# Linear attention feeding a GELU feed-forward layer: rests of two batches by head, w_out in long runs, v's cast ahead of q's last copies

## The chip, the cores and the metric

The kernel runs on one core of a Trainium2 chip. The metric is device microseconds of one execution. The kernel before took 294.98 us (median of five runs, 293.32 to 297.63). The profiled execution took 293.32 us, of which 291.54 us are the span that the trace covers.

## The reference

There are 8 batches with 8 heads, 576 tokens and a head size of 64, all in float32. Per batch and head:

```python
phi(x) = where(x > 0, x, exp(x) - 1) + 1          # = min(max(x + 1, 1), exp(x)) here
kv  = phi(k).T @ v                                  # 64 x 64
z   = sum over tokens of phi(k)                     # 64
att = (phi(q) @ kv) / (phi(q) @ z + 1e-6)
x   = att of all heads side by side                 # 4608 x 512
h   = x @ w_in                                      # w_in 512 x 2048
out = gelu_tanh(h) @ w_out                          # w_out 2048 x 512
```

The kernel leaves out the 1e-6 and computes in bfloat16 with float32 sums.

## The kernel before

**Tokens.** The 576 tokens of a batch are cut into 512 main tokens, four per partition (`C = 4`), and a rest of 64 (`REST`). Two batches share one 128-partition tile for their rests: the even batch has partitions 0 to 63, the odd one 64 to 127 (`load_rest_half`, L77). A rest is loaded with the token on the partition and the heads side by side, which in memory are runs of 64 floats, 256 bytes. Main tokens come in runs of four tokens, 1 KB (`load_main`, L65).

**kv.** Per pair of heads `kv_mm` (L222) adds five products into PSUM: four of the main chunks and one of the rest, whose v tile `vrs` is zero outside its batch's half. v carries a column of ones (`E = D + 1 = 65`), so z comes along. `kv_evac` (L243) copies the two diagonal blocks of each pair into a block-diagonal tile `kvbd`. `nab_mm` and `nab_evac` multiply q with it and divide; `t_x` transposes the result into `xt`, features on the partitions.

**Feed-forward.** The main tokens of one batch make one feed-forward pass `j` (L784), and the rests of all batches together a ninth. `first_half(j)` computes 16 feature tiles of h (`first_mm`, L307), each followed by a gelu on ScalarE into `g`; `second_half(j)` computes out from `g` and `w_out_sb` in 16 steps of four matmuls. The feature on partition p of tile m is column 128 m + p of w_in, and row 128 m + p of w_out. Both weights are loaded in float32, in 1-MB chunks of 512 features, and cast to bfloat16 mostly by POOL in halves (`cast_w_in_halves` L148, `cast_w_out_halves` L155); each w_out chunk arrives as four 2-KB runs per partition.

**Order.** The schedule is written by hand: the order in the program is the order on each engine. Work of the next batches is put into slots of `first_half` and `second_half` by `at(phase, j, slot, fn)`; a function runs behind the slot's matmuls (`fill`, L697 and L756). All plain loads ahead of the steady state go out on SP's queue, into six buffers of the pool `pld`, so a load waits until the earlier user of its buffer is done. PSUM tiles of one bank come from `ps_ho` (four), those of two banks from `ps_a` (two, taken in turn).

**The head.** Batch 0 has code of its own, L324 to L420. ScalarE computes the exponentials in halves of four heads, DVE the phi (`phi_line`, `phi_min`), TensorE the transposes of q in four pairs (`transpose_q`), with matmuls on a zero tile between (`keep_warm`). The v casts follow the last q copies, half on DVE and half on ScalarE; then kv, the products, and the first h tiles in quarters of 128 tokens.

**Batch 1** is prepared inside pass 0 by `plan_second` (L537): exponentials on ScalarE after feature tile 11, phi and v's cast on DVE at the start of the second half, q's transposes in slot 8 (first copy on ScalarE, second on DVE), kv in slot 10, the products from slot 11. The last four gelus of pass 0 stand behind these exponentials on ScalarE.

Of the kernel before, what the change touches and what calls it, by code (L numbers as in the profile page):

```python
# [15 lines left out]
def kernel(  # L16
# [40 lines left out]
    w_in_r = moe_w_in.rearrange("(c p) f -> p c f", p=P)  # L57
    w_out_r = moe_w_out.rearrange("(m p) f -> p m f", p=P)

# [37 lines left out]
    def load_w_out(i):  # L97
        t = pld.tile([P, 4, 512], FP32, name="w_st", tag="ld")
        nc.sync.dma_start(out=t, in_=w_out_r[:, 4 * i : 4 * i + 4, :])
        return t  # L100
# [14 lines left out]
    nc.scalar.preload_act_table_set("exp_and_others")  # L115
    for n, src in (("k", k), ("q", q)):
        ld[n, 0] = load_main(src, 0, n + "_x", nc.sync, parts=2)
    for n in ("kr", "vr", "qr"):
        ld[n, 0] = prest.tile([P, H, D], FP32, name=n[0] + "_r")
    load_rest_half(k, ld["kr", 0], 0, 0, nc.sync)  # L120
    load_rest_half(v, ld["vr", 0], 0, 0, nc.sync)
    ld["v", 0] = load_main(v, 0, "v_x", nc.sync, parts=2)
# [11 lines left out]
    ]  # L134
    kvbds = [const.tile([P, NP, 2 * E], BF16, name=f"kvbd{i}") for i in range(4)]
    for i in range(2):
        nc.gpsimd.memset(vps[i][:, :, :, D:E], 1.0)
        for s in range(2):
            nc.gpsimd.memset(vrs[i][s], 0.0)
            nc.gpsimd.memset(vrs[i][s][REST * s : REST * (s + 1), :, D:E], 1.0)  # L140
        nc.gpsimd.memset(kvbds[i], 0.0)
# [6 lines left out]
    def cast_w_in_halves(i):  # L148
        for u in range(2):
            nc.gpsimd.tensor_copy(  # L150
                out=w_in_sb[:, :, 512 * i + 256 * u : 512 * i + 256 * (u + 1)],
                in_=w_st[i][:, :, 256 * u : 256 * (u + 1)],
            )
# [47 lines left out]

    def exp_rest_half(name, e, s):
        r = slice(REST * s, REST * (s + 1))
        exp_into(e[r], ld[name, 0][r])

    def phi_rest_half(name, e, s):
        r = slice(REST * s, REST * (s + 1))
        phi_line(phi[name, 0][r], ld[name, 0][r])
        phi_min(phi[name, 0][r], e[r])

    def cast_v(b, fn, s=slice(0, H)):
# [5 lines left out]
    def cast_vr(m, halves=(0, 1)):  # L217
        for s in halves:
            r = slice(REST * s, REST * (s + 1))
            nc.vector.tensor_copy(out=vrs[m % 2][s][r, :, 0:D], in_=ld["vr", m][r])  # L220

    def kv_mm(b, i, kv_ps, at_i=None):  # L222
        i_ps = i if at_i is None else at_i
        kp = phi["k", b].rearrange("p c h d -> p c (h d)")
        kr = phi["kr", b // 2].rearrange("p c h d -> p c (h d)")
        dst = kv_ps[:, i_ps // 2, 2 * E * (i_ps % 2) : 2 * E * (i_ps % 2) + 2 * E]
        for c in range(C):
            nc.tensor.matmul(  # L228
                dst,
                lhsT=kp[:, c, P * i : P * (i + 1)],  # L230
                rhs=vps[b % 2][:, 2 * i : 2 * i + 2, c, :],
                start=(c == 0),
                stop=False,
            )
        nc.tensor.matmul(  # L235
            dst,
            lhsT=kr[:, 0, P * i : P * (i + 1)],
            rhs=vrs[(b // 2) % 2][b % 2][:, 2 * i : 2 * i + 2, :],
            start=False,
            stop=True,  # L240
        )

    def kv_evac(b, kv_ps, bank=None, second=None):  # L243
# [4 lines left out]
        for hf in range(2):  # L248
            r, u = slice(64 * hf, 64 * hf + 64), slice(E * hf, E * hf + E)
            fn = second if hf and second else nc.vector.tensor_copy  # L250
            fn(out=dst[r, :, :, u], in_=src[r, :, :, u])  # L251
# [73 lines left out]
    qe = pe.tile([P, C, H, D], BF16, name="q_e")  # L325
    kre = pe.tile([P, 1, H, D], BF16, name="kr_e")
    kp = pphi.tile([P, C, H, D], BF16, name="k_p")
    qp = pphi.tile([P, C, H, D], BF16, name="q_p")
    phi["k", 0], phi["q", 0] = kp, qp
    phi["kr", 0] = pphi.tile([P, 1, H, D], BF16, name="kr_p")  # L330
    nc.gpsimd.memset(phi["kr", 0][REST:P], 0.0)
    qt = pt.tile([P, C, NP, P], BF16, name="qt")
# [7 lines left out]

    def transpose_q(i, copy):
        src = q_src(0)
        t_ps = ps_ho.tile([P, C, 2, P], BF16, name="t_ps", tag="ho")
        for c in range(C):
            nc.tensor.transpose(t_ps[:, c, 0, :], src(c, i), ident)
        copy(out=qt[:, :, i, :], in_=t_ps[:, :, 0, :])

    for n, e in (("k", ke), ("q", qe)):
        for s in halves:
            exp_into(e, ld[n, 0], s)  # L350
    exp_rest_half("kr", kre, 0)
    keep_warm(36)
    for n, xp, e in (("k", kp, ke), ("q", qp, qe)):
        for s in halves:
            phi_line(xp, ld[n, 0], s)
            phi_min(xp, e, s)
    for i in range(2):
        transpose_q(i, nc.scalar.copy)
    keep_warm(5)
    phi_rest_half("kr", kre, 0)  # L360
    cast_vr(0, (0,))
    for i in range(2, NP):
        transpose_q(i, nc.scalar.copy if i == 2 else nc.vector.tensor_copy)
    keep_warm(2)
    for h in range(2):
        cast_v(0, nc.vector.tensor_copy, slice(4 * h, 4 * h + 2))
        cast_v(0, nc.scalar.copy, slice(4 * h + 2, 4 * h + 4))
    for h in range(2):
        kv_ps = ps_a.tile([P, 2, 512], FP32, name="kv_ps", tag="a")
        for i in range(2):  # L370
            kv_mm(0, 2 * h + i, kv_ps, i)
        kv_evac(0, kv_ps[:, 0:1], h, nc.scalar.copy)
    keep_warm(1)
# [54 lines left out]
    ld["k", 1] = load_main(k, 1, "k_x", nc.sync)  # L428
    load_rest_half(k, ld["kr", 0], 0, 1, nc.sync)
    wo_st.append(load_w_out(2))  # L430
    load_rest_half(v, ld["vr", 0], 0, 1, nc.sync)
    ld["v", 1] = load_main(v, 1, "v_x", nc.sync)
# [104 lines left out]
    def plan_second():  # L537
# [4 lines left out]
        def exps():  # L542
            box["q"] = pe.tile([P, C, H, D], BF16, name="q_e")
            for s in halves:
                exp_into(box["q"], ld["q", b], s)
            box["k"] = exp_main("k", b)
            box["kr"] = pe.tile([P, 1, H, D], BF16, name="kr_e")
            exp_rest_half("kr", box["kr"], 1)
            gelu_table()

        def phis():
# [4 lines left out]
            phi["k", b] = phi_of(ld["k", b], box["k"], "k_p")  # L556
            phi_rest_half("kr", box["kr"], 1)

        def cast_vs():
            cast_vr(0, (1,))  # L560
            cast_v(b, nc.vector.tensor_copy)
# [8 lines left out]
        def kv():  # L570
            kv_ps = ps_a.tile([P, 2, 512], FP32, name="kv_ps", tag="a")
            for i in range(NP):
                kv_mm(b, i, kv_ps)
            kv_evac(b, kv_ps)

        def tq(h):
# [3 lines left out]
            t_q(q_src(b), None, 2 * h, 2, t_ps)  # L580
            copy = nc.vector.tensor_copy if h else nc.scalar.copy
            copy(out=box["qt"][:, 2 * h : 2 * h + 2], in_=t_ps[:, 0:2])

# [15 lines left out]
        for fn, c, slot in (  # L599
            (tq, 0, 8), (tq, 1, 8), (lambda c: kv(), 0, 10), (lambda c: last_w_out(), 0, 10),  # L600
            (nab, 0, 11), (nab, 1, 12), (nab, 2, 13), (tx, 0, 13), (nab, 3, 14),
# [213 lines left out]
```

## Time and profile before

| what | value |
|---|---|
| median of five runs | 294.98 us |
| profiled execution | 293.32 us |
| its span | 291.54 us |
| TensorE matmuls busy | 283.5 us (97%) |
| ScalarE busy | 157.9 us (54%) |
| DVE busy | 115.1 us (39%) |
| POOL busy | 36.2 us (12%) |
| granted TensorE clock | full in all 40 slices |
| moved by DMA | 53.75 MB, mean 184 GB/s |

Times in views are microseconds from the start of the span. PE is TensorE's matmuls, PEld its weight loads, ACT ScalarE, POOL GpSimd, SP the queue that issues most loads. A timeline line gives start, length, engine, line of the code, operation, tiles and count, and in brackets how long the engine had been idle before and what released it. A matmul's recorded length is a latency: 512-column matmuls follow each other in about 0.216 us, though each is recorded with some 0.38. A busy TensorE is therefore read from its waits.

### The profile page before, as it was taken

The page shows a single profiled execution, that of the slowest core. Times are in us where ns is not written, and L with a number is a line of the kernel's source. Part 1 is how long each engine was busy: PE and PEld are TensorE (multiplying, and loading weights), DVE is VectorE, ACT ScalarE, POOL GpSimd, SP SyncE. Part 2 cuts the span into 40 slices and gives each one's busy share as a digit, 9 for nine tenths or more (in the row PEclk, how much of TensorE's full clock was granted, in tenths as well). Part 3 has the DMA queues.
Part 4 walks back from the last instruction along what each step waited for, and adds up shares of the span by engine and source line. Part 5 has one row for each costly group of instructions (what it writes and reads, how often), then busy time and mean ns, then how long its engine had stood idle before and what let it go on. Part 6 is the DMA issues. An engine that isn't in the chain of part 4 may idle for free.

```text
span 291.5 us, 4277 instructions
## 1 busy us (share of the span) xinstructions
PE 283.5 (97%) x1693; PEld 149.4 (51%) x1722; DVE 115.1 (39%) x187; ACT 157.9 (54%) x219; POOL 36.2 (12%) x56
## 2 busy tenths in 40 slices
PE   8999999999999999999999999999999999999994
PEld 6885446645565545544454445444544444444443
DVE  3760586146683792447035642462240000000012
ACT  4647684589855753566356925672551076026400
POOL 8057338400007000000000000000000000000000
PEclk9999999999999999999999999999999999999999
DMA  6999999995389995998923894305150110020032
GB/s 238 355 406 397 367 365 382 342 366 159 68 262 215 323 196 150 290 255 291 329 56 70 296 266 112 72 3 160 53 74 18 72 74 0 31 94 21 0 72 72
DMA packets 65907, 53.75 MB, mean 184 GB/s; under 512 B 33888, under 2 KB 58720, under 8 KB 65888
## 3 DMA queue, kind: packets, MB, share of 16 engines
q1 hardware_dynamic: 62464, 42.35, 52.2%
q10 hardware_dynamic: 2464, 8.52, 7.5%
q0 software_dynamic: 960, 2.62, 3.0%
q8 instruction: 13, 0.21, 0.3%
q14 instruction: 6, 0.05, 0.0%
HBM read 36.70 MB, written 9.44 MB: 158 GB/s over the span
## 4 chain that ended last, share of the span: by engine, by line
PE 84%; DMA 7%; SPq 5%; POOL 1%; issue 1%; DVE 1%; DVEq 0%
PE o_ps L738 39%; PE h_ps L310 38%; DMA w_st<-in_moe_w_in_dram 4%; DMA w_st<-in_moe_w_out_dram 3%; PE n_ps L262 3%; PE kv_ps L228 2%; SPq L78 2%; SPq L69 2%; PE o_ps L707 1%; SPq L92 1%; POOL w_in_sb L150 1%; PE kv_ps L235 1%; POOL w_out_sb L157 0%; PE t_ps L285 0%; PE t_ps L256 0%
## 5 line engine op out<-in xcount | busy, mean ns | idle before, releaser
L738 PE MATMUL o_ps<-w_out_sb,g 128*128 128x512 bf16 x547 | 123.3, 379 | 1.0 <-POOL w_out_sb L157 0.3
L310 PE MATMUL h_ps<-xt,w_in_sb 128*128 128x512 bf16 (+2 forms) x574 | 118.5, 351 | 0.8
L695 ACT ACTIVATE g<-h_ps 128x512 bf16<-128x512 f32 x144 | 84.1, 598 | 49.4 <-PE h_ps L310 48.0
L738 PEld LDWEIGHTS <-g 128*128 128x128 bf16 x560 | 54.2, 98 | 63.6 <-issue 0.5
L310 PEld LDWEIGHTS <-w_in_sb 128*128 128x128 bf16 x652 | 59.1, 98 | 53.6 <-issue 0.3
L753 ACT COPY o_sb<-o_ps 128x512 f32<-128x512 f32 x18 | 10.5, 586 | 58.4 <-PE o_ps L738 58.4
L751 DVE COPY o_sb<-o_ps 128x512 f32<-128x512 f32 x17 | 11.7, 689 | 66.3 <-PE o_ps L738 59.0
L274 DVE TENSOR_TENSOR x<-n_ps,r 128x512 bf16<-128x512 f32 x36 | 24.9, 692 | 1.2
L251 DVE CAST kvbd<-kv_ps 64x260 bf16<-64x260 f32 (+1 forms) x16 | 6.6, 410 | 36.7 <-PE kv_ps L235 36.6
L169 ACT ACTIVATE k_e<-k_x 128x2048 bf16<-128x2048 f32 (+1 forms) x9 | 15.5, 1719 | 4.7 <-DMA k_x<-in_k_dram 4.7
L272 DVE RECIPROCAL r<-n_ps 128x8 f32<-128x8 f32 x36 | 7.4, 206 | 24.9 <-PE n_ps L262 24.9
L169 ACT ACTIVATE q_e<-q_x 128x2048 bf16<-128x2048 f32 (+1 forms) x10 | 15.5, 1559 | 2.5 <-DMA q_x<-in_q_dram 2.5
L186 DVE TENSOR_TENSOR k_p<-k_p,k_e 128x2048 bf16<-128x2048 bf16 (+1 forms) x9 | 10.0, 1106 | 12.3 <-ACT k_e L169 12.0
L180 DVE TENSOR_SCALAR q_p<-q_x 128x2048 bf16<-128x2048 f32 (+1 forms) x10 | 11.6, 1156 | 8.0 <-DMA q_x<-in_q_dram 7.9
L337 PE MATMUL w_ps<-warm 128*128 128x252 bf16 x94 | 13.4, 306 | 1.1 <-DVE warm L128 1.1
L310 PE MATMUL h_ps<-xt_rest,w_in_sb 128*128 128x512 bf16 x62 | 13.9, 379 | 0.1
L262 PEld LDWEIGHTS <-qt 128*128 128x128 bf16 x128 | 9.8, 98 | 7.5 <-DVE kvbd L251 0.6
L262 PE MATMUL n_ps<-kvbd,qt 128*128 128x130 bf16 x128 | 12.7, 221 | 0.4 <-ACT kvbd L251 0.2
L186 DVE TENSOR_TENSOR q_p<-q_p,q_e 128x2048 bf16<-128x2048 bf16 (+1 forms) x10 | 10.6, 1061 | 6.0 <-ACT q_e L169 5.4
L212 DVE CAST vp<-v_x 128x2048 bf16<-128x2048 f32 (+1 forms) x9 | 9.3, 1045 | 8.6 <-DMA v_x<-in_v_dram 8.6
L228 PEld LDWEIGHTS <-k_p 128*128 128x128 bf16 x128 | 9.5, 96 | 6.0 <-DVE vp L212 0.7
L228 PE MATMUL kv_ps<-vp,k_p 128*128 128x130 bf16 x128 | 11.7, 220 | 0.4 <-DVE vp L212 0.4
(52 smaller groups left out, 136.3 us busy)
## 6 DMA issues: line engine op xcount, KB each, us to landing
out_dram<-o_sb ACTq DMA_DIRECT2D x16, 512.0 KB, 3.9
k_x<-in_k_dram SPq DMA_DIRECT2D x7, 1024.0 KB, 10.1
v_x<-in_v_dram SPq DMA_DIRECT2D x7, 1024.0 KB, 11.5
q_x<-in_q_dram SPq DMA_DIRECT2D x6, 1024.0 KB, 8.5
w_st<-in_moe_w_in_dram SPq DMA_DIRECT2D x4, 1024.0 KB, 10.1
w_st<-in_moe_w_out_dram SPq DMA_DIRECT2D x4, 1024.0 KB, 11.0
q_x<-in_q_dram SPq DMA_DIRECT2D x4, 512.0 KB, 9.8
k_x<-in_k_dram SPq DMA_DIRECT2D x2, 512.0 KB, 4.1
```

Of the source, the lines that this page charges most:

```text
L169: nc.scalar.activation(e[:, :, hs, :].rearrange("p c h d -> p h c d"), by_chunk(x[:, hs]), AF.Exp)
L180: nc.vector.tensor_scalar(xp[:, :, hs, :].rearrange("p c h d -> p h c d"), by_chunk(x[:, hs]), 1.0, 1.0, op0=ALU.add, op1=ALU.max,)
L186: nc.vector.tensor_tensor(xp[:, :, hs, :], xp[:, :, hs, :], e[:, :, hs, :], op=ALU.min)
L228: nc.tensor.matmul(dst, lhsT=kp[:, c, P * i : P * (i + 1)], rhs=vps[b % 2][:, 2 * i : 2 * i + 2, c, :], start=(c == 0), stop=False,)
L262: nc.tensor.matmul(n_ps[rows, i // 2, 2 * E * (i % 2) : 2 * E * (i % 2) + 2 * E], lhsT=qt_c[:, i, rows], rhs=kvbd[:, i, :], skip_group_che ...
L274: nc.vector.tensor_tensor(x, n_v[:, :, :, 0:D], r[:, :, :, None].to_broadcast([P, 2, 4, D]), op=ALU.mult,)
L310: nc.tensor.matmul(h_ps[:, tok], lhsT=w_in_sb[:, c, P * m : P * (m + 1)], rhs=xt[:, c, tok], start=(c == 0), stop=(c == KM - 1), skip_grou ...
L337: nc.tensor.matmul(w_ps[:, 0:252], lhsT=warm[:, 0:P], rhs=warm)
L695: nc.scalar.activation(gs[j][:, i, :], ps, AF.Gelu_apprx_tanh)
L738: nc.tensor.matmul(o_pss[t], lhsT=g[:, m, P * t : P * (t + 1)], rhs=w_out_sb[:, m, :], start=(m == 0), stop=(m == MM - 1),)
L751: nc.vector.tensor_copy(dst, o_ps)
L753: nc.scalar.copy(dst, o_ps)
```

## The change

Four things change, all of them in the first 55 us.

1. **Rests of k and v of batches 0 and 1.** They are loaded with the head and a group of four tokens on the partition (`load_rest_by_head`): partition 8 g + h holds tokens 4 g to 4 g + 3 of head h, one run of 1 KB. k's rest and v's rest go out on SP ahead of q (batch 0) and side by side behind k (batch 1). To keep heads apart, v is multiplied with a mask per pair of heads (`mask_vrh`, four activations on ScalarE with a per-partition scale) and phi(k) with a mask of odd and even heads (`phi_krh`, DVE); both masks are made from the identity matrix at the start. The masked tiles lie in a buffer of `g`'s pool, so the buffers of `g` change places. Per batch the rest takes eight matmuls in place of four: in batch 0 they come first and start the sum, with 260 columns; in batch 1 they go to a PSUM tile of their own in slot 9 (`kv_rests`), ScalarE copies it to SBUF, and `kv_evac` adds it.
2. **w_out** is read in runs of 8 KB: partition p takes four rows that follow each other. The feature order of g changes with it, and so the cast of w_in gathers every fourth column.
3. **Batch 0's order.** v's casts stand between q's copies; kv's PSUM tiles are taken earlier, and fewer warm-up matmuls are issued (32 in front for 36, 1 for 7 behind).
4. **Batch 1** has both copies of q's transposes on ScalarE.

```diff
-    w_out_r = moe_w_out.rearrange("(m p) f -> p m f", p=P)
+    w_out_r = moe_w_out.rearrange("(i p m) f -> i p m f", p=P, m=4)
...
+    G = P // H
+    def load_rest_by_head(b):
+        for n, src in (("kr", k), ("vr", v)):
+            nc.sync.dma_start(
+                out=rest_by_head(n, b).rearrange("p c d -> p (c d)"),
+                in_=src[b, :, MAIN:S, :].rearrange("h (g c) d -> g h (c d)", g=G),
+            )
...
+    ld["k", 0] = load_main(k, 0, "k_x", nc.sync, parts=2)
+    load_rest_by_head(0)
+    ld["q", 0] = load_main(q, 0, "q_x", nc.sync, parts=2)
     ld["v", 0] = load_main(v, 0, "v_x", nc.sync, parts=2)
...
             nc.gpsimd.tensor_copy(
-                out=w_in_sb[:, :, 512 * i + 256 * u : 512 * i + 256 * (u + 1)],
-                in_=w_st[i][:, :, 256 * u : 256 * (u + 1)],
+                out=w_in_sb[
+                    :, :, 512 * i + 256 * u : 512 * i + 256 * (u + 1)
+                ].rearrange("p c (m x) -> p c m x", m=2),
+                in_=w_st[i].rearrange("p c (x m) -> p c m x", m=4)[
+                    :, :, 2 * u : 2 * u + 2
+                ],
             )
...
+    def mask_vrh(b, pairs):
+        for i in pairs:
+            nc.scalar.activation(
+                vrh[b][:, :, i, 0:D], rest_by_head("vr", b), AF.Copy,
+                scale=pair[:, i : i + 1],
+            )
+    def phi_krh(b):
+        e, line, kr = krh[b]
+        nc.vector.tensor_scalar(
+            line[:, :, 0], rest_by_head("kr", b), 1.0, 1.0, op0=ALU.add, op1=ALU.max
+        )
+        nc.vector.tensor_tensor(line[:, :, 0], line[:, :, 0], e[:, :, 0], op=ALU.min)
+        for t in range(2):
+            nc.vector.tensor_scalar(
+                kr[:, :, t], line[:, :, 0], odd[:, t : t + 1], None, op0=ALU.mult
+            )
...
+    for t in halves:
+        exp_into(ke, ld["k", 0], t)
+    exp_krh(0)
+    mask_vrh(0, (0, 1))
+    for u, t in enumerate(halves):
+        exp_into(qe, ld["q", 0], t)
+        mask_vrh(0, (2 + u,))
+    keep_warm(32)
...
+    copy_q[0](nc.scalar.copy)
+    cast_v(0, nc.vector.tensor_copy, slice(0, 2))
+    cast_v(0, nc.scalar.copy, slice(2, 4))
+    copy_q[1](nc.vector.tensor_copy)
+    copy_q += [transpose_q(2), transpose_q(3)]
+    cast_v(0, nc.vector.tensor_copy, slice(4, 6))
+    cast_v(0, nc.scalar.copy, slice(6, 8))
+    copy_q[3](nc.vector.tensor_copy)
+    copy_q[2](nc.scalar.copy)
...
-    load_rest_half(k, ld["kr", 0], 0, 1, nc.sync)
+    load_rest_by_head(1)
     wo_st.append(load_w_out(2))
-    load_rest_half(v, ld["vr", 0], 0, 1, nc.sync)
...
-            phi_rest_half("kr", box["kr"], 1)
+            phi_krh(1)
+            mask_vrh(1, range(NP))
...
-            kv_evac(b, kv_ps)
+            kv_evac(b, kv_ps, second=box["rests"])
+        def kv_rests():
+            r_ps = ps_a.tile([P, 2, 512], FP32, name="r_ps", tag="a")
+            for a in range(2):
+                kv_mm_rests(b, a, r_ps[:, a, 0 : 2 * E])
+            ...
+            nc.scalar.copy(box["rests"], ...)
...
-            copy = nc.vector.tensor_copy if h else nc.scalar.copy
-            copy(out=box["qt"][:, 2 * h : 2 * h + 2], in_=t_ps[:, 0:2])
+            nc.scalar.copy(out=box["qt"][:, 2 * h : 2 * h + 2], in_=t_ps[:, 0:2])
...
-            (tq, 0, 8), (tq, 1, 8), (lambda c: kv(), 0, 10), (lambda c: last_w_out(), 0, 10),
+            (tq, 0, 8), (tq, 1, 8), (lambda c: kv_rests(), 0, 9), (lambda c: kv(), 0, 10), (lambda c: last_w_out(), 0, 10),
```

## The prediction

> **What bounds the kernel now.** I read the chain that ended last, then the waits of TensorE after the head, then the timeline of the first 55 us, then the same time in windows of 1 us. The chain (shares of the span) and, from 55 us to the end, the only wait of TensorE (us in total, times, longest):
>
> ```profile
> PE 84%; DMA 7%; SPq 5%; POOL 1%; issue 1%; DVE 1%; DVEq 0%
> PE o_ps L738 <- issue: 0.2, 1, 0.2
> ```
>
> So from 55 us on TensorE is full: 0.2 us of waits in 236 us. The change leaves that work alone, so what it is worth is read at one point: the first product of batch 1 with its kv (L262, 46.24 us before). Whatever this start moves by, the end moves by. The timeline up to it (start, length, engine, line, tiles, idle before and its releaser):
>
> ```profile
> 10.40 1.06 ACT L169 ACTIVATE q_e<-q_x 128x1024 bf16<-128x1024 f32 x1 [1.22 <-DMA q_x<-in_q_dram]
> 13.33 0.42 DVE L346 COPY qt<-t_ps 128x512 bf16<-128x512 bf16 x1
> 13.58 1.14 ACT L212 CAST vp<-v_x 128x512 bf16<-128x512 f32 x2
> 16.15 0.51 PE L262 MATMUL n_ps<-kvbd,qt 128*128 128x130 bf16 x6 [0.24 <-ACT kvbd L251]
> 16.85 2.02 POOL L150 CAST w_in_sb<-w_st 128x1024 bf16<-128x1024 f32 x2 [9.09 <-DMA w_st<-in_moe_w_in_dram]
> 18.76 0.61 PE L310 MATMUL h_ps<-xt,w_in_sb 128*128 128x128 bf16 x8
> ...
> 35.74 1.91 ACT L169 ACTIVATE k_e<-k_x 128x2048 bf16<-128x2048 f32 x1 [1.94 <-DMA k_x<-in_k_dram]
> 39.38 2.22 POOL L157 CAST w_out_sb<-w_st 128x1024 bf16<-128x1024 f32 x2 [4.41 <-DMA w_st<-in_moe_w_out_dram]
> 39.62 2.06 ACT L695 ACTIVATE g<-h_ps 128x512 bf16<-128x512 f32 x4
> 40.48 1.02 PE L738 MATMUL o_ps<-w_out_sb,g 128*128 128x512 bf16 x4 [0.26 <-POOL w_out_sb L157]
> 41.98 1.01 ACT L582 COPY qt<-t_ps 128x1024 bf16<-128x1024 bf16 x1 [0.30 <-PE t_ps L256]
> 46.24 0.41 PE L262 MATMUL n_ps<-kvbd,qt 128*128 128x130 bf16 x4
> ```
>
> Useful matmuls begin at 18.76. ScalarE is late too: it waits for k of batch 1 until 35.74, so the last gelus end at 41.68. The windows (busy share of PE, PEld, DVE, ACT, POOL; clock; DMA share; GB/s) show what the rests cost:
>
> ```profile
> 8.00:9.00 1.00, 1.00 (x11) 0.91 (x10) 0.79 (x2) 0.88 (x1) 0.00 (x0) 1.00 1.22 312
> 9.00:10.00 1.00, 1.00 (x12) 0.91 (x10) 0.69 (x1) 0.18 (x1) 0.00 (x0) 1.00 1.17 231
> 13.00:14.00 1.00, 0.72 (x10) 0.42 (x7) 1.00 (x5) 0.90 (x2) 0.00 (x0) 1.00 1.07 415
> ```
>
> The DMA engines are full; where the 256-byte runs of k's and v's rests pass, the rate falls from some 400 GB/s to 312 and 231.
>
> **DMA.** Batch 0's rests lose (400-312)+(400-231) = 257 KB, 0.64 us; by the single packets (256 bytes take 18 to 20 ns, 1 KB 46 ns, and 1-KB neighbours stretch to 60 and more) it is 0.9. I take 0.8: the first w_in chunk lands at 16.05, not 16.85. w_out: 2-KB packets take 84 ns, the stores' 4-KB ones 159, so a 1-MB chunk gains between 0 and 0.2 us; I take 0.2. k of batch 1 lands 35.74-0.8-0.4 (two w_out chunks ahead of it), and some 0.3 less since its last packets no longer pass among rests: 34.25. Its bounds are 35.7 (nothing gained) and 33.7. The third w_out chunk, now behind v's rest too (0.3), has one more chunk and both slow rests off its path: about 37.7 instead of 39.33. On SP's queue k's and v's rests now stand ahead of q: q's first half lands about 0.7 later (8.8), while its second half, which formerly shared the engines with the rests, stays near 10.1 to 10.4.
>
> **Batch 0 up to its kv.** ScalarE gets exp of k's rest and four masks in place of one kr exp of 0.61. A 128x512 cast takes 0.62 and a 128x1024 exp 1.06, so 128x256 is 0.42. Here a rule is weighed: the Trainium skill, ScalarE: Activation LUTs, section What ACT_TABLE_LOAD costs, says that a per-partition scale adds about 93 ns to an activation and that neighbours overlap by as much. By the rows four masks take 1.68, by the rule between 1.7 and 2.0 (no row has such a scale); I take 1.7. Exp and two masks fill ScalarE's 1.28 idle us ahead of q; the last two stand behind q's halves: q_e ends 11.35, mask 11.75. DVE gets five short operations (odd, pair before the data; some 1.1 us of phi of the rest while it waits for q); phi of q ends at 12.1, as before (12.18). TensorE gets eight rest matmuls of 260 columns (0.11 each, 0.9) instead of four of 130, while it would run warm-up. Then the new order counts: v's first casts 12.1 to 12.85 rather than after the q copies (13.58), the others 12.9 to 13.4, q's last copies to 14.0, the four kvbd copies in turn to 14.9 (0.3 each). The products with kv start at 14.95, not 16.15: 1.2 earlier, hence first_mm could start at 17.5.
>
> **w_in's cast.** POOL now reads every fourth float. No row shows such a read; the nearest is L150 itself at 1.04 us for 1024. The Trainium skill speaks against the change: GPSIMD Engine Reference, section Performance pitfalls for Q7 kernels, puts a read whose step is over 8 bytes (here 16) at about 2.9 cycles an element against 1.9. As a ratio on the row that is 1.56 us a cast; as 2.9 cycles at its 1.2 GHz, 2.47; a gain is excluded, since the elements are as many. I take 1.56, the ratio, because the row is already faster than the page's lower figure, and keep 1.04 and 2.47 as ends. At 1.56: halves ready at 17.6 and 19.2, against uses at 18.71 and 19.43 before. TensorE gains 1.1 on the first and 0.25 on the second, and keeps 0.25 through h of batch 0. The last w_in half is ready at 28.5, and TensorE needs it at 31.4: hidden. SP's loads of w_out and of k, v of batch 1 wait for those buffers, but each is released 3 us or more ahead of its turn on the full DMA queue.
>
> **Batch 1, where the gain goes.** ScalarE: k_e 34.25 to 36.15, exp of the rest 0.42 (was 0.63), table 1.28, four gelus 2.06: the gelus end at 39.95, 1.73 earlier. But then come four masks, 1.7, and only behind them the copy of the first q transposes, 1.01: done at 42.7. TensorE's new rest matmuls sit one slot after these transposes and write the PSUM buffer that this copy frees. TensorE, which would reach them at about 42.3 (i=8 at 39.6, transposes, i=9), stands until 42.7; in the best case of the casts it would be there at 41.5 and stands 1.2. Behind the standing matmul are all of o_ps, kv and the products. From there: 8 matmuls 0.5, i=10 0.86, kv 16 x 0.058 = 0.93, DVE's two adds into kvbd 0.95 with their waits (as L251's 0.87): 46.0. The second q copy, moved from DVE to ScalarE (1.01), ends at 43.7 and frees kv's buffer (needed at 44.1); the copy of the rests' product follows at 44.1; w_out's half cast ends at 45.2 and is first used after 46.9. DVE's phi of the rest and v's cast (v landed by 40.5) end by 42.4 even if POOL holds each up as it does now (L220 took 1.26 instead of 0.42): needed at 44.1.
>
> **Sum.** 46.24 - 46.0 = 0.24 us gained; the first output tile and g's buffers only change places. The profiled execution had 293.32 (span 291.54 and 1.8 around it), so 293.1; the median of the runs lies 1.66 above it: 294.8. A measurement of this kernel tells about 1% (2.95 us) from no change.
>
> **Rivals.**
> *The strided cast is slow* (slower). Eight casts from 16.05 on end at 16.05+8X, and the last two feature tiles take 1.73 more; before, this ended at 33.14. Up to X = 1.92 us nothing is lost, then every 0.1 costs 0.8; at 2.29 the loss is 1%. At 2.47 h ends at 37.5, 4.4 late; ScalarE's masks are then hidden and the start of batch 1 is at 50.2: 4.0 slower, 299. For: the cited rule, and 16 bytes is well past its step. Against: the contiguous row at 1.04 is not what the page has for its own base.
> *The ScalarE queue doesn't bind* (faster). k lands at 33.3 or the masks are shorter, and TensorE keeps the head's 1.2: 293.6. For: k's landing carries most of the DMA gain, and a median execution has more DMA delay to lose than the profiled one. Against: ScalarE has q's exps until 32.6 to 33.8 anyway. More than 1.7 isn't there: w_in's first half can't be ready before 17.1.
> *Longer runs don't help*, HBM being the limit: k lands as before, the gelus end at 41.5, masks and copy at 44.2: the start is at 47.5, 1.3 slower, 296.2. Against it stand the 312 and 231 GB/s.
>
> **Numbers.** Main case 0.45 (294.2 to 295.5), slow cast 0.28, of which 0.25 beyond 1%, ScalarE not binding 0.17, of which 0.06 beyond 1% since medians spread, no DMA gain 0.10. Faster 0.06, within 0.67, slower 0.27. The range takes in most of the fast rival and the slow cast up to 2.47: 293.4 to 299.0; leaving 0.04 below and some 0.14 above.
>
> **What would show it.** L195 on POOL: mean near 1.56, wrong above 1.9. First h_ps matmul near 17.6. k_e of batch 1 at 34.2. In TensorE's waits the first matmul into r_ps standing up to 1 us for ScalarE's q copy; if it doesn't stand, the forecast gain is too small. L264's mean near 0.42. The windows at 6 to 10 us at about 380 GB/s without the dip. The forecast is wrong if POOL becomes what TensorE waits for between 19 and 37 us.

## The result

Over 43 executions the changed kernel has a median of 293.49 us (293.11 to 294.07), the kernel before 294.46 over 78 beside it (293.07 to 297.63). Two further executions of the kernel before, at 431.05 and 610.99 us, are far slower than all others and are left out. The ratio is 0.9965, with a 95% interval of 0.9955 to 0.9974: about 1.0 us less, within the 1% that the prediction called no change. The time predicted, 294.8 (293.4 to 299.0), was 1.3 us too high, near the other end of its range.

The two lists of times differ in one way only. The fastest executions are equal (293.07 and 293.11). But a quarter of those before lie above 295.07 (quartiles 293.95 and 295.07), while after the change the quartiles are 293.33 and 293.64. The change took away a spread; it made no execution faster than the best before. The profiles say the same: the profiled execution of before had 293.32, the fifth fastest of its 78, and that of after has 293.71. In the profiles the change is 0.4 us **slower**.

The chain that ended last in the changed kernel, and TensorE's waits from 17 to 55 us (total, times, longest); from 55 us on it waits for nothing:

```profile
PE 84%; DMA 6%; DVE 6%; SPq 1%; issue 1%; ACT 1%; DVEq 0%
```

```profile
PE h_ps L392 <- POOL w_in_sb L195: 1.1, 1, 1.1
PE n_ps L344 <- DVE kvbd L328: 0.2, 1, 0.2
```

Of the kernel before, in the same stretch:

```profile
PE t_ps L285 <- DVE x L274: 0.4, 1, 0.4
PE o_ps L738 <- POOL w_out_sb L157: 0.3, 1, 0.3
```

TensorE is as full as before; there is a new wait of 1.1 us, for the cast of w_in. The timeline of the changed kernel (start, length, engine, line, tiles, idle before and its releaser; groups that matter less are left out):

```profile
8.03 1.06 ACT L218 ACTIVATE q_e<-q_x 128x1024 bf16<-128x1024 f32 x1
10.17 1.06 ACT L218 ACTIVATE q_e<-q_x 128x1024 bf16<-128x1024 f32 x1 [0.68 <-DMA q_x<-in_q_dram]
...
14.51 0.91 PE L344 MATMUL n_ps<-kvbd,qt 128*128 128x130 bf16 x8
15.51 15.77 POOL L195 CAST w_in_sb<-w_st 128x1024 bf16<-128x1024 f32 x8 [7.36 <-DMA w_st<-in_moe_w_in_dram]
17.58 0.62 PE L392 MATMUL h_ps<-xt,w_in_sb 128*128 128x128 bf16 x8
19.52 1.07 PE L392 MATMUL h_ps<-xt,w_in_sb 128*128 128x128 bf16 x16 [1.10 <-POOL w_in_sb L195]
...
27.59 8.17 DVE L229 TENSOR_SCALAR q_p<-q_x 128x1024 bf16<-128x1024 f32 x1 [6.31 <-DMA q_x<-in_q_dram]
31.20 4.01 POOL L206 CAST w_out_sb<-w_st 128x1024 bf16<-128x1024 f32 x4
...
34.74 1.91 ACT L218 ACTIVATE k_e<-k_x 128x2048 bf16<-128x2048 f32 x1 [0.84 <-DMA k_x<-in_k_dram]
...
38.27 2.07 ACT L800 ACTIVATE g<-h_ps 128x512 bf16<-128x512 f32 x4
38.33 3.63 POOL L206 CAST w_out_sb<-w_st 128x1024 bf16<-128x1024 f32 x2 [3.12 <-DMA w_st<-in_moe_w_out_dram]
40.20 1.73 ACT L264 ACTIVATE g<-v_r,pair 128x256 bf16<-128x256 f32 x4
41.80 1.93 ACT L687 COPY qt<-t_ps 128x1024 bf16<-128x1024 bf16 x2
42.54 0.48 DVE L280 TENSOR_SCALAR g<-g,odd 128x256 bf16<-128x256 bf16 x2
43.08 0.63 PE L287 MATMUL r_ps<-g 128*128 128x130 bf16 x8
...
46.57 0.41 PE L344 MATMUL n_ps<-kvbd,qt 128*128 128x130 bf16 x4 [0.20 <-DVE kvbd L328]
```

Read it from the top. All eight first products with kv of batch 0 run from 14.51 on (before two at 15.64 and the other six at 16.15), w_in lands at 15.51 instead of 16.85, and the first useful matmul is at 17.58 instead of 18.76. So far everything is 1.2 us or more ahead. Then the second w_in half isn't there: its matmuls start at 19.52, against 19.43 before (in the view of before: `19.43 1.06 PE L310 MATMUL h_ps<-xt,w_in_sb 128*128 128x128 bf16 x16`), and the whole gain of the head is gone on one wait. The eight casts run back to back (15.77 us for eight), so POOL is what sets this. Later k of batch 1 and the third w_out chunk are 1.0 ahead (34.74 for 35.74, 38.33 for 39.38), ScalarE's masks and q copy stand behind the gelus, and the first product of batch 1, at which the prediction read the change's worth, is at 46.57 instead of 46.24. Near 43 TensorE stands once more. The four o_ps matmuls from 41.91 on take 0.86 us (0.216 each), but the first matmul into r_ps comes 1.17 us after the group's start, since its weights wait for DVE's masked phi (L280), which ends at 43.02, late by way of the operation of 8.17 us:

```profile
43.08 0.46 PEld L287 LDWEIGHTS <-g 128*128 128x128 bf16 x8 [0.64 <-DVE g L280]
```

The windows of 1 us in which the rests passed before (busy shares of PE, PEld, DVE, ACT, POOL; clock; DMA share; GB/s):

```profile
7.00:8.00 1.00, 1.00 (x12) 0.91 (x10) 0.90 (x3) 1.00 (x3) 1.00 (x2) 1.00 0.94 285
8.00:9.00 1.00, 1.00 (x12) 0.91 (x10) 0.86 (x5) 1.00 (x3) 0.15 (x1) 1.00 1.05 363
9.00:10.00 1.00, 1.00 (x11) 0.91 (x10) 0.90 (x4) 0.49 (x2) 0.00 (x0) 1.00 1.04 366
```

The 312 and 231 GB/s between 8 and 10 us are now 363 and 366, but between 7 and 8 us, where the kernel before had 374, there is now a dip to 285.

### The profile page after: what moved, and what is told of

Its sections match the earlier page's. It is cut to its first block, busy times and chain, and to the rows that moved or that the text cites. A ratio compares the mean times of both kernels' runs of the same rounds, so it can differ in the third digit from the quotient of the medians.

```text
span 291.9 us, 4269 instructions
## 1 busy us (share of the span) xinstructions
PE 283.0 (97%) x1681; PEld 148.4 (51%) x1710; DVE 120.5 (41%) x191; ACT 161.1 (55%) x228; POOL 44.9 (15%) x57
## 4 chain that ended last, share of the span: by engine, by line
PE 84%; DMA 6%; DVE 6%; SPq 1%; issue 1%; ACT 1%; DVEq 0%
PE o_ps L843 38%; PE h_ps L392 37%; DMA q_x<-in_q_dram 6%; DVE q_p L229 3%; PE n_ps L344 3%; PE kv_ps L301 2%; PE o_ps L812 1%; DVE k_p L235 1%; SPq L69 1%; DVE q_p L235 0%; PE kv_ps L312 0%; SPq L124 0%; DVE k_p L229 0%; ACT q_e L218 0%; DVE g L275 0%
## 5 line engine op out<-in xcount | busy, mean ns | idle before, releaser
L229 DVE TENSOR_SCALAR q_p<-q_x 128x2048 bf16<-128x2048 f32 (+1 forms) x10 | 17.6, 1757 | 6.4 <-DMA q_x<-in_q_dram 6.3
L333 DVE CAST kvbd<-kv_ps 64x260 bf16<-64x260 f32 (+1 forms) x14 | 5.7, 408 | 35.0 <-PE kv_ps L312 34.7
L195 POOL CAST w_in_sb<-w_st 128x1024 bf16<-128x1024 f32 x8 | 15.8, 2036 | 7.4 <-DMA w_st<-in_moe_w_in_dram 7.4
L235 DVE TENSOR_TENSOR k_p<-k_p,k_e 128x2048 bf16<-128x2048 bf16 (+1 forms) x9 | 10.6, 1179 | 11.9 <-ACT k_e L218 11.4
L416 PE MATMUL w_ps<-warm 128*128 128x252 bf16 x74 | 11.5, 323 | 1.1 <-DVE warm L141 1.1
L229 DVE TENSOR_SCALAR k_p<-k_x 128x2048 bf16<-128x2048 f32 (+1 forms) x9 | 10.6, 1173 | 2.6 <-DMA k_x<-in_k_dram 2.6
```

Source lines behind the costliest of these rows:

```text
L195: nc.gpsimd.tensor_copy(out=w_in_sb[:, :, 512 * i + 256 * u : 512 * i + 256 * (u + 1)].rearrange("p c (m x) -> p c m x", m=2), in_=w_st[i] ...
L229: nc.vector.tensor_scalar(xp[:, :, hs, :].rearrange("p c h d -> p h c d"), by_chunk(x[:, hs]), 1.0, 1.0, op0=ALU.add, op1=ALU.max,)
L235: nc.vector.tensor_tensor(xp[:, :, hs, :], xp[:, :, hs, :], e[:, :, hs, :], op=ALU.min)
L416: nc.tensor.matmul(w_ps[:, 0:252], lhsT=warm[:, 0:P], rhs=warm)
```

## The experiments

They ran on three chips, each beside runs of the kernel before on the same chip (medians there 294.81, 294.15 and 294.44), so the ratios are compared rather than the times. Where profiles are compared, the first w_in cast, the first h matmul and the first product of batch 1 are the marks. The last of them holds what the prediction read from it: in 13 of the 14 profiled executions the whole time is 247.05 to 247.14 us more than the start of that product (246.72 in the kernel without two of the loads, below). So what moves this start moves the end by as much.

### The w_out part, taken out and alone

The changed kernel with w_out loaded in 2-KB runs, and w_in's cast contiguous again:

```diff
-    w_out_r = moe_w_out.rearrange("(i p m) f -> i p m f", p=P, m=4)
+    w_out_r = moe_w_out.rearrange("(m p) f -> p m f", p=P)
...
-                ].rearrange("p c (m x) -> p c m x", m=2),
-                in_=w_st[i].rearrange("p c (x m) -> p c m x", m=4)[
-                    :, :, 2 * u : 2 * u + 2
-                ],
+                in_=w_st[i][:, :, 256 * u : 256 * (u + 1)],
```

> The changed kernel with w_out back in 2-KB runs and w_in's cast contiguous again. In the changed kernel the gathering cast takes 2.0 us and starves DVE (one q_p operation of batch 1 lasts 8.2 us), so TensorE's rest products of batch 1 stand for DVE. Theory A (the gathering cast takes the head's gain away, and long runs give little): casts at 1.04, first h tiles go on at 17.6 without the 1.1 us wait, DVE free by 41, products of batch 1 at 45.6 to 46.1 instead of 46.57, median 0.4 to 1.0 us below the changed kernel. Theory B (the long runs carry the gain of the median, by the earlier w_out chunks): products of batch 1 at 46.5 or later, since k and the third w_out chunk land about 0.5 later, and the median 0.5 or more above the changed kernel.

Measured: 293.66 us, ratio 0.9964 (0.9947 to 0.9981), the same as the changed kernel. TensorE's waits from 17 to 60 us in its profile:

```profile
PE r_ps L283 <- ACT qt L683: 0.9, 1, 0.9
PE o_ps L839 <- POOL w_out_sb L202: 0.3, 1, 0.3
PE n_ps L340 <- DVE kvbd L324: 0.2, 1, 0.2
```

The wait for w_in is gone, and in its place TensorE stands 0.9 us for ScalarE's copy of q. That is the wait that the prediction had named for the changed kernel. There it had not shown, because TensorE, held at 19 us, came to r_ps that much later. In this profile ScalarE is also later by itself: k's exp of batch 1 starts at 35.24 instead of 34.74, as k landed later. With the one wait taken away, the other took the time.

The kernel before, with only w_out's 8-KB runs and the strided cast (its loads up to w_in are those of before):

```diff
-        nc.sync.dma_start(out=t, in_=w_out_r[:, 4 * i : 4 * i + 4, :])
+        nc.sync.dma_start(out=t, in_=w_out_r[i])
...
-                in_=w_st[i][:, :, 256 * u : 256 * (u + 1)],
+                in_=w_st[i].rearrange("p c (x m) -> p c m x", m=4)[
+                    :, :, 2 * u : 2 * u + 2
+                ],
```

> The kernel before with only w_out in 8-KB runs and the gathering cast of w_in. Theory A: the casts at 2.0 us make it slower: w_in's first half ready at 18.9, the second at 20.9 instead of 18.9, TensorE 1.5 us late from there, DVE starved as in the changed kernel: 1.5 to 2.5 us above the kernel before. Theory B: the third w_out chunk lands about 0.6 earlier and the spread of the runs (293 to 297) narrows to that of the changed kernel: median 0 to 0.7 below the kernel before.

Measured: 295.39 us, ratio 1.0038 (1.0017 to 1.0058): 0.6 us above its chip's median, 1.1 by the ratio; slower, as theory A has it, but by less than its 1.5 to 2.5. Its cast, and TensorE's wait for it:

```profile
L150 POOL CAST w_in_sb<-w_st 128x1024 bf16<-128x1024 f32 x8 | 16.2, 2079 | 10.0 <-DMA w_st<-in_moe_w_in_dram 10.0
```

```profile
PE h_ps L314 <- POOL w_in_sb L150: 1.1, 1, 1.1
```

So this part is a loss by itself. The strided cast costs 2.08 us a piece where the contiguous one has 1.0, and the 1.1 us wait is the same as in the changed kernel.

### What made the spread: the head

The kernel before, profiled once more:

> The kernel before once more, for another profiled execution: the first was one of its fastest (293.32 against a median of 294.51 over 80 runs, while the changed kernel's 43 runs stay within 293.11 to 294.07). If an execution of 294.5 or more is caught, theory C (late loads: the spread is the time that TensorE waits for the third w_out chunk, k or v of batch 1) expects waits of TensorE in 17 to 55 us longer than the 0.7 us of the first by as much as the time is longer; theory D (the head or the tail varies) expects the same waits there and the difference before 17 us or after 55 us.

Its profiled execution took 293.75, again one of the shorter ones; w_in landed at 16.95. An execution of 294.5 or more was not caught, but the two profiles already differ by 0.43 us, and the difference is in the head, as theory D has it: q's exps start at 8.74 and 10.93 instead of 8.12 and 10.40, the first h matmul at 19.24 instead of 18.76, and the first product of batch 1 at 46.66 instead of 46.24. Next, the kernel before with nothing but v's casts put ahead of q's later copies:

```diff
-        copy(out=qt[:, :, i, :], in_=t_ps[:, :, 0, :])
+        return lambda copy: copy(out=qt[:, :, i, :], in_=t_ps[:, :, 0, :])
...
+    copy_q[0](nc.scalar.copy)
+    cast_v(0, nc.vector.tensor_copy, slice(0, 2))
+    cast_v(0, nc.scalar.copy, slice(2, 4))
+    copy_q[1](nc.vector.tensor_copy)
```

> The kernel before with only v's casts of batch 0 put ahead of q's copies, as in the changed kernel; rests, w_out and batch 1 as they were. v lands at about 13.5 here, so the casts can't be earlier than 12.6 and 13.6: first products of batch 0 at 15.2 to 15.6 instead of 16.15, w_in's first half ready at 17.9, so first h tiles 0.8 earlier at most. Theory A says that this small head gain is lost where TensorE waits for the third w_out chunk (landing 39.33): its wait grows from 0.3 to about 1, products of batch 1 within 0.2 of 46.24, median within 0.3 of the kernel before. If the head's gain reached the end, the median would be 0.6 to 0.8 lower.

Measured: 293.75 us (292.95 to 297.47), ratio 0.9968 (0.9941 to 0.9996). The products with kv come at 15.19 instead of 15.64, the first h matmul at 18.25; but then TensorE waits 1.4 us for the third w_out chunk, as theory A expected, and the first product of batch 1 comes at 46.87: in this execution nothing of the head's gain is left. The median is lower than that theory allowed, though 3 of the 12 executions lie at 295.0, 295.65 and 297.47 (the ratio is taken without the last). So the spread stays, and whether the order of v's casts gains by itself is not settled.

The kernel before without the loads of batch 0's rests of k and v: this one leaves out a part of the computation, since the tokens of those two rests are replaced by a constant.

```diff
-    load_rest_half(k, ld["kr", 0], 0, 0, nc.sync)
-    load_rest_half(v, ld["vr", 0], 0, 0, nc.sync)
+    for n in ("kr", "vr"):
+        nc.gpsimd.memset(ld[n, 0][0:REST], 0.5)
```

> The kernel before without the loads of batch 0's rests of k and v (their tiles are filled with a constant instead, so that part of the result is left out); all else as before. Seen so far: in four profiled executions with the 256-byte rests behind q, q's first half is there at 7.96 to 9.76 and its second at 10.17 to 11.39, and the time follows the first h tiles (18.76 and 293.32, 19.24 and 293.75). Theory R (the rests' packets behind q delay q by an amount that varies from execution to execution, and that is the spread of the kernel before): q at 7.4 to 8.0 and 9.3 to 9.9, w_in 1.3 earlier, median 0.8 to 1.5 below the kernel before and most runs within 0.8 of each other. Theory S (the spread comes from elsewhere, and the changed kernel only absorbs it in later waits): the median falls by at most 0.5 and the runs still spread over 2 us or more.

Measured: 292.63 us (291.99 to 293.05), ratio 0.9934 (0.9911 to 0.9957). The spread is gone: all 12 executions lie within 1.1 us. So those two small loads, 128 KB each, made it. In the one profiled execution q's halves were not early (9.07 and 10.84, where less than 8.0 had been expected for the first), so q's landing alone is not what the loads delay.

Is it the length of their runs or their place? The kernel before with the same 256-byte loads, moved ahead of q on SP's queue:

```diff
-    for n, src in (("k", k), ("q", q)):
-        ld[n, 0] = load_main(src, 0, n + "_x", nc.sync, parts=2)
+    ld["k", 0] = load_main(k, 0, "k_x", nc.sync, parts=2)
     for n in ("kr", "vr", "qr"):
         ld[n, 0] = prest.tile([P, H, D], FP32, name=n[0] + "_r")
     load_rest_half(k, ld["kr", 0], 0, 0, nc.sync)
     load_rest_half(v, ld["vr", 0], 0, 0, nc.sync)
+    ld["q", 0] = load_main(q, 0, "q_x", nc.sync, parts=2)
```

> The kernel before with the same 256-byte loads of batch 0's rests put ahead of q, as in the changed kernel; only the order on the queue. If the order makes the difference, q is there as regularly as in the changed kernel (8.1 and 10.2) and the spread is that of the changed kernel. If the length of the runs does, the rests now hold up both halves of q: 9 to 10 and 11, first h tiles 0.3 to 1 later than 18.76, median equal to the kernel before or up to 1 above it, with its spread.

Measured: 292.83 us (292.36 to 293.22), ratio 0.9953 (0.9931 to 0.9975). With not a byte loaded otherwise, the place on the queue takes the spread away. That the length of the runs had to change is refuted: by that theory this kernel should have been level with before or up to 1 us slower. A kernel with 1-KB runs left behind q was not run, so whether longer runs alone would have done it too is open. Over all kernels here with the rests ahead of q, 1 of 122 executions lies above 295 us (295.43); of the kernel before, 45 of 164. Both orders together, that is the edits of the last diff and of v's casts in one kernel, still in 256-byte runs and without masks:

> The kernel before with two moves of lines and nothing else: the rests of batch 0 (256-byte runs, unmasked) ahead of q on SP's queue, and v's casts ahead of q's later copies. Against the change to batch 0 alone it differs in the run length, the masks and the way the rests enter kv. Theory 'order': within 0.3 us of batch 0 alone (ratio near 0.993). Theory 'length': q and v land 0.7 us later behind 256-byte runs, so 0.5 to 0.9 us above it (ratio 0.995 to 0.996, no better than the rests' order alone).

Measured: 292.73 us (292.44 to 293.14), ratio 0.9935 (0.9915 to 0.9955). On the same chip the part of the change for batch 0 alone, with its 1-KB runs and masks, had 292.93 (below). So two moves of lines give all of the gain that batch 0's part has, and more than the whole change. What the second move adds to the first is not shown: the profiled execution with the first alone took 292.77, that with both 292.83.

What goes with the place is seen in one window, 5 to 12 us, the last column being the mean GB/s. Of the kernel before, of its second profile, of v first and of w_out's part alone, all four with the rests behind q:

```profile
5.00:12.00 7.00, 7.00 (x67) 6.23 (x65) 5.19 (x8) 4.24 (x6) 2.65 (x5) 1.00 1.07 323
```

```profile
5.00:12.00 7.00, 7.00 (x69) 6.31 (x67) 4.70 (x7) 3.73 (x5) 2.67 (x5) 1.00 1.07 303
```

```profile
5.00:12.00 7.00, 7.00 (x70) 6.36 (x68) 5.35 (x9) 4.50 (x6) 2.67 (x5) 1.00 1.10 314
```

```profile
5.00:12.00 7.00, 5.97 (x59) 5.22 (x58) 4.46 (x7) 3.27 (x4) 2.67 (x5) 1.00 1.08 294
```

Of the rests ahead of q in 256-byte runs, of both orders, and of the changed kernel:

```profile
5.00:12.00 7.00, 7.00 (x69) 6.30 (x67) 5.55 (x9) 4.85 (x7) 2.63 (x4) 1.00 1.12 354
```

```profile
5.00:12.00 7.00, 7.00 (x66) 6.20 (x64) 5.38 (x9) 4.52 (x6) 2.70 (x5) 1.00 1.11 345
```

```profile
5.00:12.00 7.00, 6.71 (x59) 5.58 (x57) 6.42 (x13) 5.91 (x11) 3.03 (x6) 1.00 1.05 357
```

Behind q the four executions moved 294 to 323 GB/s, ahead of it 345 and 354, and the changed kernel 357 (359 to 372 in the six other profiles with 1-KB runs ahead of q). Over 7 us the means of the two groups with 256-byte runs (308 and 350) are 290 KB apart, 0.7 us at 400 GB/s, for the same loads; 1-KB runs add 0.1 to 0.4 us on top, which the times don't show. But the window alone doesn't tell which kernel spreads: without the rests it moved no more than before.

```profile
5.00:12.00 7.00, 6.79 (x68) 5.99 (x66) 4.80 (x8) 3.86 (x5) 3.55 (x7) 1.00 0.99 329
```

SP goes with the place too. With the rests behind q it takes 3.4 to 4.6 us to issue v's two loads, and the first load of w_in is issued at 8.1 to 9.4; with the same 256-byte runs ahead of q it takes 1.6, and w_in follows at 6.4. Of the kernel before and of the rests ahead of q:

```profile
4.69 3.53 SPq L69 DMA_DIRECT2D v_x<-in_v_dram  x2
```

```profile
4.74 1.60 SPq L69 DMA_DIRECT2D v_x<-in_v_dram  x2
```

Since the DMA engines are full meanwhile, this may be a cause or only a consequence. The execution with 294 GB/s had w_in at 17.77 and the first h matmul at 19.85, and took 295.51: this is what one of the longer executions looks like, though here in a kernel that has the strided cast too. No such execution of the kernel before itself was profiled. Why the same small loads cost more when q is already on the queue ahead of them is not shown by these traces.

### Batch 1

The change to batch 0 alone: w_out's 2-KB runs, the contiguous cast, and batch 1's rests loaded, cast and multiplied as before (in short):

```diff
-    load_rest_by_head(1)
+    load_rest_half(k, rest1["kr"], 0, 1, nc.sync)
+    load_rest_half(v, rest1["vr"], 0, 1, nc.sync)
...
-            mask_vrh(1, range(NP))
...
-            kv_evac(b, kv_ps, second=box["rests"])
+            kv_evac(b, kv_ps)
...
-            nc.scalar.copy(out=box["qt"][:, 2 * h : 2 * h + 2], in_=t_ps[:, 0:2])
+            copy = nc.vector.tensor_copy if h else nc.scalar.copy
+            copy(out=box["qt"][:, 2 * h : 2 * h + 2], in_=t_ps[:, 0:2])
```

> The changed kernel with w_out in 2-KB runs and batch 1 as in the kernel before (256-byte rests, one rest product per pair, one of q's copies on DVE, no masks): only batch 0's part is kept. Theory A (batch 0's part carries all of the gain, and batch 1's masks and extra copy on ScalarE cost part of it): the wait of 0.9 for ScalarE's q copy is gone, products of batch 1 at 45.4 to 45.8, median 0.8 to 1.3 below the 2-KB variant of the changed kernel (293.66) and 1.5 to 2.2 below the kernel before. If batch 1's rests in 1-KB runs were needed too: the third w_out chunk lands at 39.3 or later, products at 46.2 or later, median not below 293.5, with outliers to 296.

Measured: 292.40 us (291.95 to 292.56), ratio 0.9926 (0.9896 to 0.9956). In its profile the first h matmul is at 17.71, nothing stands at 19 us, and the first product of batch 1 comes 1.2 us before that of the changed kernel:

```profile
45.41 0.41 PE L335 MATMUL n_ps<-kvbd,qt 128*128 128x130 bf16 x4 [0.17 <-DVE kvbd L324]
```

The other way round the wait for ScalarE: the changed kernel with w_out's part taken out, batch 1's rests loaded ahead of its k, and their exp and masks ahead of k's exp on ScalarE:

```diff
-    ld["k", 1] = load_main(k, 1, "k_x", nc.sync)
     load_rest_by_head(1)
+    ld["k", 1] = load_main(k, 1, "k_x", nc.sync)
...
-            box["k"] = exp_main("k", b)
             exp_krh(1)
+            mask_vrh(1, range(NP))
+            box["k"] = exp_main("k", b)
```

> The changed kernel with w_out in 2-KB runs and batch 1's rests loaded ahead of its k, so that exp of the rest and the four masks run on ScalarE while it waits for k. Theory A: the gelus of pass 0 end at about 41.2 (k lands 0.7 later), q's first copy follows at once, TensorE does not stand for the rest products (0.9 before), products of batch 1 at 45.8 to 46.2, median 0.6 to 1.0 below the 2-KB variant (293.66). Rival: the later k moves the gelus so far that the transposes of q stand for their PSUM buffers, and the time stays within 0.3.

Measured: 293.01 us, ratio 0.9949 (0.9927 to 0.9971). ScalarE is no longer waited for; the third w_out chunk is:

```profile
PE o_ps L839 <- POOL w_out_sb L202: 1.3, 1, 1.3
```

It has the earliest head of all (first h matmul at 17.06) and can't use it: TensorE then arrives before w_out does. In the two profiles of batch 0 alone (the second is below) the same wait is 0.4 and 0.9.

Last, on one chip, the changed kernel again, batch 0 alone again, and the changed kernel with only batch 1 put back, which keeps w_out's part (its diff is that of batch 0 alone, without the lines on w_out):

> The changed kernel itself, beside the three others on one chip. Ratio to the kernel before 0.9965, as shown (0.9955 to 0.9974); a profile with w_in's casts at 1.97 to 2.04 us, TensorE waiting about 1.1 us for the second half of w_in, and one DVE operation of several us (8.2 in the profile shown) between 19 and 28 us. If that DVE operation is short this time and the time is the same, it costs nothing; if it is short and the time is 0.5 us lower, DVE is what was last.

> The change to batch 0 alone, again, so that it stands on the same chip as the changed kernel. If batch 1's masks and w_out's runs cost what the earlier ratios say (0.9926 against 0.9964), it lies 1.1 us below the changed kernel; if that was the difference between two chips, it lies within 0.4 us of it.

> The changed kernel with only batch 1's rests put back as before (w_out's 8-KB runs and the strided cast of w_in stay). Theory 'two costs that add': TensorE still waits 1.1 us for POOL near 19 us, but not for DVE's rest or ScalarE's copies, so it lies 0.4 to 0.7 us below the changed kernel and as much above batch 0 alone. Theory 'one hides the other': whatever is lost at 19 us on POOL is the whole loss, and it equals the changed kernel within 0.2 us.

Measured: the changed kernel 293.57 us, ratio 0.9971 (0.9954 to 0.9989); with batch 1 put back 293.18, 0.9956 (0.9934 to 0.9978); batch 0 alone 292.93, 0.9963 (0.9933 to 0.9994; a single execution of 295.43 makes its interval wide, its profiled one took 292.44). So batch 1's part costs 0.4 us and w_out's part some 0.25 more by the medians, 0.45 and 0.7 by the profiled executions (293.57, 293.12, 292.44). The theory of two costs had 0.4 to 0.7 for each. But the wait of 1.1 us that it named is not in the profile with batch 1 put back: there an operation of DVE in the head took 2.26 us (L229, at 6.20), the first h matmul came at 18.24, and TensorE stood 0.3 for the second w_in half, which let it go on at 19.17. Batch 0 alone lies 0.64 below the changed kernel by the medians, between the 1.1 and the 0.4 of its two readings. The costs don't add freely: with batch 1's part in place, taking w_out's part out gained nothing (0.9964 beside 0.9965), as ScalarE's wait came in its place. The intervals overlap, so the single steps are likely, not certain; that both together cost is what the profiles and both runs of batch 0 alone agree on.

In the changed kernel's second profile the long DVE operation was short, and DVE's work for the rests was done before ScalarE's copy:

```profile
27.49 2.17 DVE L229 TENSOR_SCALAR q_p<-q_x 128x1024 bf16<-128x1024 f32 x1 [6.41 <-DMA q_x<-in_q_dram]
...
41.52 0.48 DVE L280 TENSOR_SCALAR g<-g,odd 128x256 bf16<-128x256 bf16 x2
41.86 1.93 ACT L687 COPY qt<-t_ps 128x1024 bf16<-128x1024 bf16 x2
42.97 0.62 PE L287 MATMUL r_ps<-g 128*128 128x130 bf16 x8
...
46.44 0.41 PE L344 MATMUL n_ps<-kvbd,qt 128*128 128x130 bf16 x4 [0.20 <-DVE kvbd L328]
```

The first of the two copies ends near 42.8, where the prediction had 42.7. TensorE comes to r_ps at 42.97 and stands neither for it nor for DVE. It had lost that time before: the eighth cast of w_in took 2.49 us here instead of 2.0, and the last feature tiles of h waited for it.

```profile
29.05 2.49 POOL L195 CAST w_in_sb<-w_st 128x1024 bf16<-128x1024 f32 x1
31.59 1.41 PEld L392 LDWEIGHTS <-w_in_sb 128*128 128x128 bf16 x8 [0.60 <-POOL w_in_sb L195]
```

The stretch from 20.45 to the first o_ps at 33.33 is 12.88 us long, where the first profile has 12.59 (20.65 to 33.24). So each profile has a second loss of some 0.3 us: the first for DVE near 43, this one for POOL near 31.6, and the start of batch 1 differs by only 0.13, the time by 0.14. The late last cast is also in the profiles of w_out's part alone (weights waiting 0.56 until 34.02) and with batch 1 put back (0.61 until 31.44).

## Why the prediction was right and where it was wrong

That the change stays within 1% was right, but in part by luck. The mechanism that it named, a gain at the head that is given back, is there; in the profiles more than the gain is given back, 0.4 us slower where 0.2 faster was forecast. That the medians lie 1.0 us apart has another cause, which it did not have. Two of its own signs of being wrong came true, L195 above 1.9 and POOL as what TensorE waits for at 19 us, and the windows from 6 to 10 us have 285 to 366 GB/s instead of 380 without a dip. The errors, by its steps:

- **Sum** is the step that failed. It took the 1.66 between the profiled execution and the median of before as a constant and added it to the forecast of after. In the changed kernel the two lie at 293.71 and 293.49, and in its second profile at 293.57 for both: the difference is -0.2 and 0.0, so the term was 1.7 to 1.9 too large. The forecast of the profiled execution, 293.1, was 0.5 to 0.6 too low, so the time came out only 1.3 too high. Of the 1.66, 0.5 was the choice of five runs (294.98; 294.46 over 78). The rest was spread, made by the rests behind q in the loads of the head, and a part of the change removes it (shown by the rests-first kernel and by the one without those loads). The prediction's fast rival said that "a median execution has more DMA delay to lose than the profiled one" and did not give it a number.
- **DMA**: the new place of the rests was booked as a cost, q's first half landing 0.7 later at 8.8. Its exp started at 8.03, when ScalarE came free, not later than before (8.12); in the second profile at 8.25. w_in gained 1.34 (1.55 in the second profile) where 0.8 was taken. k of batch 1 landed at 34.74 instead of 34.25, the third w_out chunk at 38.33 instead of 37.7: the 0.2 for each chunk in 8-KB runs was too much. Counted from the first w_in cast, k's exp starts 19.23, 19.34 and 19.40 us later with 8-KB runs (the changed kernel twice, batch 1 put back) and 19.18, 19.53 and 19.60 with 2-KB runs (batch 0 alone twice, w_out's part taken out): 0.1 in the mean for both chunks ahead of it together, within the scatter.
- **Batch 0 up to its kv** held: products at 14.51 (forecast 14.95), first h matmul at 17.58 (17.6), a mask 0.43 (0.42). The rows named there give 0.40 for 128x256, not 0.42, and k's exp of that size did take 0.40. A mask by itself took 0.49 to 0.50, four in a row 1.73: that fits the rule weighed there, 0.09 more for the scale and as much hidden between neighbours.
- **w_in's cast** is mis-sized: 1.97 to 2.04 us instead of 1.56, above the 1.9 that the prediction called wrong. By the ratio of the Trainium skill's GPSIMD Engine Reference, section Performance pitfalls for Q7 kernels, it should have been 1.56, by its absolute 2.9 cycles 2.47; the case lies between. The extra 1.0 us over the contiguous 1.04 is about 1.2 cycles an element at that page's clock, so the page's *difference* between strided and contiguous is nearest, put on this trace's base rather than multiplied. The forecast of where it hurts was also off. Eight casts ending too late cost nothing in the first profile (they end at 31.28, as w_in landed early) and 0.3 us in the second (31.53). But the second half came at 19.5 and 19.3, so TensorE kept nothing of the head where 0.25 had been forecast.
- **Batch 1, where the gain goes** named the right mechanism. Gelus ended at 40.34 (39.95), four masks took 1.73 (1.7), the first q copy ended near 42.8 (42.7), and without w_out's part TensorE stood 0.9 for it. In the changed kernel ScalarE's copy costs it nothing, since it comes to r_ps itself only at 42.8 and 43.0; the 0.3 that it stood in the first profile was for DVE. That DVE's phi of the rest and v's cast end by 42.4 even if POOL holds each up failed in the first profile (43.0), through the 8.17 us operation, and held for the phi in the second (42.0); v's cast ended at 44.2 and 43.1. Together the start of batch 1 is at 46.57 and 46.44 instead of 46.0.

Of the rivals, the slow cast came half true: past its threshold of 1.92, yet not a loss of 1% or more. That the ScalarE queue doesn't bind is what happened for another reason than its own (its 293.6 is near the 293.49 measured, by chance), and longer runs that do not help was nearly right for the run *length*: what helped was the order that came with them.

## What to carry to other kernels

Before a profiled execution is used as a baseline, see where it stands among the other times: here it was the fifth fastest of 78, and the change's whole worth was in the others. When a change rewrites a load, part its place on the queue from its form and try the move of lines alone; two such moves gave 0.65% here, where the whole change with masks and longer runs gave 0.29% on the same chip. A gain early in a kernel is worth only what the next supplier can follow: TensorE, 1.2 us early, met a cast at 19 us, or ScalarE's copy, or w_out's third chunk, one behind the other. Faster than both kernels are the change to batch 0 alone (0.9926 and 0.9963) and the two moves of lines (0.9935).

## What the runs showed of the hardware

A DVE operation lasted 8.17 us in the changed kernel (L229 at 27.59, shown with the result). The same operation on the other half of q took 0.69 there:

```profile
36.47 0.69 DVE L229 TENSOR_SCALAR q_p<-q_x 128x1024 bf16<-128x1024 f32 x1
```

The long one began while POOL's strided casts ran back to back until 31.28; POOL went on with w_out's casts to 35.21, and DVE's operation ended 0.55 us after that, which is nearly its own length. In the three other profiles with strided casts (the changed kernel again, w_out's part alone, batch 1 put back) it took 2.17, 2.03 and 1.97 us, and ended 0.55 us after POOL's seventh cast; the eighth, beginning meanwhile, took 2.49 or 2.50 instead of 2.0. Where POOL's casts are contiguous, with pauses between their pairs, it took 0.90 to 1.48. The Trainium skill, SBUF — State Buffer, section SBUF: two separate sides, says that the two engines share a pair of ports that one holds for a whole instruction while the other blocks. The three profiles agree with that in both directions: DVE waits out one cast, and the next cast waits out DVE. 8.17 us would mean that DVE lost its turn to several casts in a row, once in four executions. That it was this lock is inferred from the times and was not tested, and why DVE lost its turn only once is open.

Two loads of 128 KB in 256-byte runs, behind q on the same queue, made the whole kernel's time spread over 3.7 us on one chip (292.94 to 296.63, 31 executions); ahead of q, the same loads left 0.9 us there (12 executions), and a median 1.3 us lower (294.15 and 292.83).
